# One ring of four double PSUM buffers in the attention stage, paired maxima, and regrouped weight steps

## The chip, the cores and the metric

The kernel runs on one core of a Trainium2 chip. The core has five engines with queues of their own: TensorE (PE in the profile, its weight loads PEld), VectorE (DVE), ScalarE (ACT), GpSimd (POOL) and SyncE (SP, which only issues transfers here). TensorE writes its results into PSUM, which has eight banks of 512 fp32 numbers in each of 128 partitions; the other engines read them there. The metric is the device time of one execution in microseconds (us), lower is better.

## The reference

```python
def _attn_ref(q, k, v):                     # 2 x 8 heads, 1152 keys, head_dim 64
    q_pool = q.reshape(B, H, S // 2, 2, D).mean(axis=3)      # 576 queries
    scores = scale * np.matmul(q_pool, k.transpose(0, 1, 3, 2))
    scores = scores - np.max(scores, axis=-1, keepdims=True)
    attn = np.exp(scores)
    attn = attn / (np.sum(attn, axis=-1, keepdims=True) + 1e-09)
    return np.matmul(attn, v)
...
x = attn_out                                # 1152 tokens x 512
g = np.maximum(x @ w_in, 0.0) ** 2          # 512 -> 2048
x = g @ w_out                               # 2048 -> 512
return (x @ w_a) * (x @ w_b) @ w_out2       # 512 -> 1536 -> 512
```

The weights are float64 and q, k, v float32; the output is float32.

## The kernel before

fp32 products are made of pieces: a number x is split into `hi` (x rounded to fp32r by ScalarE) and `lo` (x minus hi, by VectorE), and a product is hi·hi + hi·lo + lo·hi. float64 weights are brought to fp32 on the chip by integer operations (`w_stage`).

**Units.** Attention runs over 8 pairs of heads p (tile halves of 64 partitions, one head each) and two halves of the 576 queries: 16 units n = 2p + c of 288 queries. A unit does this, and the order in which the code is written is the order on every engine, since the schedule is manual:

- `scores(n, t)` for nine blocks of 128 keys: eight matmuls of 288 columns into one double buffer `ps` (a bank for each head); the last two add the negated row maxima (`mrow`). ScalarE makes `e` = exp(ps), and GpSimd adds the `e` up (`acc`; in the last unit VectorE does). VectorE adds the last two blocks (`sum_last`), GpSimd adds that to `acc` at the start of the next unit (`sum_end`).
- Between the score rounds, `max_pair(p+1, j, c)` makes scores of the *next* pair, for the row maxima alone: two matmuls of 384 columns (one head each), and VectorE reduces each to a column (`colmax`). There are six such pairs in a unit, nine in unit 1, none in units 14 and 15.
- `prep(p+2, odd)` transposes the keys and queries of the pair after the next into `pt` and splits them: 8 blocks in even units, 7 in odd ones (none from unit 12 on). `max_row` transposes the maxima (`mr`, copied to `mrow` by ScalarE). In odd units `max_mix` makes three more matmuls for maxima of the last queries.
- `values(n)`: 36 matmuls e·v into `po`; ScalarE copies the result to `xf`.
- `scale(n-2)`: VectorE's reciprocal of the sums `sg` and the product with `xf`. `denom(n-1)`: `acc` summed over partitions by TensorE (`den`), copied to `sg` by ScalarE. `x_split(n-3)` splits the finished output into `xh` and `xl`.
- In units 12 to 15, `w_step` prepares the first four weight tiles in three stages each: stage 0 is L129 (ScalarE) and L131 (VectorE), stage 1 is L135 and L138 (VectorE) and, at the next step, L119 (ScalarE), stage 2 is L153 (VectorE).

After unit 15, `early_mm(f)` and `early_post(f)`, f = 0 to 3, make the first products of the feed-forward part (tiles `e`, 24 matmuls of 288 columns each) from outputs of the first batch, into buffers of the same PSUM pool; ScalarE frees them with `r` (L563). Then come the two feed-forward parts, in which TensorE is busy nearly without a gap.

**Start.** Before unit 0 the keys of pair 0 come in three blocks of 384 (`pk`): three transposes, `prep_hi`, three `max_pair`, `prep_lo`. Then `max_end`, `prep(1, 0)`, `prep(1, 1)` and `max_row(0)`.

**PSUM.** Two pools share the eight banks:

```python
ps_s = es.enter_context(tc.tile_pool(name="ps_s", bufs=2, space=PSUM))
ps_m = es.enter_context(tc.tile_pool(name="ps_m", bufs=4, space=PSUM))
```

`ps_s` has two double buffers (`two_banks`): `ps`, `pt`, `po`, `pk` and the early products `e`. `ps_m` has four single ones: the scores for maxima `pm`, `mr` and `den`. A new tile takes a buffer of its pool that is free in program order, and its first matmul waits until the last reader of the old tile is done. Which instruction waits for which is fixed when the program is built: before, score round t waits for the exponential of round t-2, and a pair of `pm` for the maxima of two pairs earlier.

## Time and profile before

| | |
|---|---|
| time, median of 3 runs | 678.01 us (676.39 to 678.29) |
| the profiled execution | 679.79 us, of which 677.6 us is the span of the trace |
| TensorE busy in the span | 659.6 us (97%) |
| VectorE, ScalarE, GpSimd busy | 456.2, 310.5 and 195.9 us |
| attention up to the first early product | 245.3 us of the span |
| transfers | 52.90 MB, 78 GB/s on average |

Busy time of TensorE counts a matmul from its start to the modelled end of its pipeline, so that it overlaps with the next; it shows a short wait hardly at all. What TensorE lost is read from the starts of its instructions in the timeline, and from the granted clock, which has two levels here: 1.00 (2.4 GHz) and half of it (1.2 GHz).

### The profile page before, as it was taken

What the parts mean: (1) busy time and instruction counts of PE and PEld (TensorE: products, weight loads), DVE (VectorE), ACT (ScalarE), POOL (GpSimd) and SP (SyncE); (2) the same over time, 40 slices, a digit from 0 to 9 for tenths busy, and PEclk for the clock granted to TensorE, in tenths of its full rate; (3) what the DMA queues carried; (4) which work ended last, traced back from release to release, by engine and by line L of the source; (5) the groups of instructions that cost most, each with busy time, mean ns of one, the idle gap of its engine ahead of it and who ended that gap; (6) DMA issues with size and microseconds to landing.
All of it is one profiled execution on the core that took longest, in us unless ns stands there. A gap on an engine that the chain in (4) does not pass through costs nothing.

```text
span 677.6 us, 11443 instructions
## 1 busy us (share of the span) xinstructions
PE 659.6 (97%) x4614; PEld 586.2 (87%) x4614; DVE 456.2 (67%) x808; ACT 310.5 (46%) x571; POOL 195.9 (29%) x157
## 2 busy tenths in 40 slices
PE   6999999999998989999999999999999999999997
PEld 4777777777766669999999999999999889999986
DVE  5777888888799796894249874576777312777311
ACT  1454566566654745672247652334555222555100
POOL 1477889889887610320000000000000000000000
PEclk8699999999998998999999999999999999999999
DMA  7704034041031120322224321323434210441022
GB/s 174 176 1 106 12 96 107 1 105 37 2 129 32 33 63 27 123 86 86 85 62 125 95 63 62 94 94 94 125 124 127 91 31 1 124 125 63 17 63 62
DMA packets 55541, 52.90 MB, mean 78 GB/s; under 512 B 20416, under 2 KB 49344, under 8 KB 55488
## 3 DMA queue, kind: packets, MB, share of 16 engines
q1 hardware_dynamic: 55280, 51.58, 26.9%
q8 instruction: 36, 0.59, 0.4%
q10 hardware_dynamic: 208, 0.59, 0.3%
q14 instruction: 17, 0.14, 0.1%
HBM read 49.81 MB, written 2.36 MB: 77 GB/s over the span
## 4 chain that ended last, share of the span: by engine, by line
PE 89%; DVE 6%; ACT 3%; DMA 1%; issue 0%; ACTq 0%; DVEq 0%
PE ps L374 12%; PE po L400 9%; PE y L546 5%; PE y L544 5%; PE y L545 5%; PE h L546 4%; PE h L544 4%; PE h L545 4%; PE a L544 4%; PE b L544 4%; PE a L545 4%; PE b L545 4%; PE a L546 4%; PE b L546 4%; PE o L545 4%; PE o L546 4%
## 5 line engine op out<-in xcount | busy, mean ns | idle before, releaser
L386 POOL TENSOR_TENSOR acc<-acc,e 128x576 f32<-128x576 f32 x75 | 107.8, 1437 | 5.9
L318 DVE TENSOR_REDUCE mm<-pm 128x1 f32<-128x384 f32 x192 | 93.9, 549 | 18.9 <-PE pm L325 18.4
L379 ACT ACTIVATE e<-ps 128x576 f32<-128x576 f32 x144 | 92.7, 652 | 28.5 <-PE ps L374 23.9
L153 DVE TENSOR_TENSOR wlo<-wx,whi 128x512 fp32r<-128x512 f32 x60 | 42.4, 707 | 54.2 <-ACT whi L119 54.2
L400 PE MATMUL po<-e,vin 128*64 128x288 f32 x576 | 73.4, 409 | 0.0
L119 ACT CAST whi<-wx 128x512 fp32r<-128x512 f32 x68 | 42.2, 620 | 60.6 <-DVE wx L138 60.6
L544 PE MATMUL y<-gh,whi 128*128 128x384 f32 x192 | 64.6, 336 | 0.0
L546 PE MATMUL y<-gh,wlo 128*128 128x384 f32 x192 | 64.5, 336 | 0.0
L545 PE MATMUL y<-gl,whi 128*128 128x384 f32 x192 | 64.5, 336 | 0.0
L400 PEld LDWEIGHTS po<-e,vin 128*64 128x64 f32 x576 | 39.9, 137 | 27.7 <-issue 1.5
L374 PE MATMUL ps<-hi 64*128 64x288 f32 x288 | 55.2, 365 | 2.9 <-ACT e L379 1.6
L546 PE MATMUL h<-xh,wlo 128*128 128x384 f32 (+1 forms) x176 | 57.5, 327 | 0.0
L545 PE MATMUL h<-xl,whi 128*128 128x384 f32 (+1 forms) x176 | 57.5, 327 | 0.0
L544 PE MATMUL h<-xh,whi 128*128 128x384 f32 (+1 forms) x176 | 57.5, 327 | 0.0
L687 DVE TENSOR_TENSOR t<-b,as 128x384 f32<-128x384 f32 x36 | 20.1, 558 | 46.2 <-PE b L546 46.2
L138 DVE SCALAR_TENSOR_TENSOR wx<-raw,wx 128x512 int32<-128x512 int32 x68 | 49.3, 725 | 2.4
L374 PEld LDWEIGHTS ps<-hi 64*128 64x128 f32 x288 | 28.7, 189 | 23.3 <-ACT e L379 14.8
L546 PE MATMUL a<-yh,wlo 128*128 128x384 f32 x144 | 48.1, 334 | 0.0
L544 PE MATMUL a<-yh,whi 128*128 128x384 f32 x144 | 48.1, 334 | 0.0
L545 PE MATMUL a<-yl,whi 128*128 128x384 f32 x144 | 48.1, 334 | 0.0
L544 PE MATMUL b<-yh,whi 128*128 128x384 f32 x144 | 48.1, 334 | 0.0
L545 PE MATMUL b<-yl,whi 128*128 128x384 f32 x144 | 48.1, 334 | 0.0
(109 smaller groups left out, 1592.0 us busy)
## 6 DMA issues: line engine op xcount, KB each, us to landing
raw<-in_moe_w_out_dram SPq DMA_DIRECT2D x28, 512.0 KB, 3.4
raw<-in_moe_w_in_dram SPq DMA_DIRECT2D x16, 512.0 KB, 3.8
raw<-in_moe_w_a_dram SPq DMA_DIRECT2D x12, 512.0 KB, 3.5
raw<-in_moe_w_b_dram SPq DMA_DIRECT2D x12, 512.0 KB, 3.6
vin<-in_v_dram SPq DMA_DIRECT2D x8, 576.0 KB, 4.2
qin<-in_q_dram SPq DMA_DIRECT2D x7, 576.0 KB, 6.3
kin<-in_k_dram SPq DMA_DIRECT2D x14, 288.0 KB, 5.3
out_dram<-oacc SPq DMA_DIRECT2D x5, 192.0 KB, 2.2
```

The lines of the kernel that those rows point to most:

```text
L119: nc.scalar.copy(w["hi"], w["x"].bitcast(F32))
L138: nc.vector.scalar_tensor_tensor(out=x, in0=high.bitcast(I32), scalar=-(2 ** 31), in1=x, op0=ALU.bitwise_and, op1=ALU.bitwise_or)
L153: eng.tensor_tensor(out=lo, in0=x.bitcast(F32), in1=hi.bitcast(F32), op=ALU.subtract)
L318: nc.vector.tensor_reduce(out=mm[p][:, i, c:c + 1], in_=ps[:, :MC], op=ALU.max, axis=AX.X)
L374: nc.tensor.matmul(ps[:, a, :CQ], w, m, start=i == 0, stop=i == 3)
L379: nc.scalar.activation(ex[u, t], ps[:, :, :CQ], AF.Exp, scale=SCALE)
L386: eng.tensor_tensor(out=acc[u], in0=acc[u], in1=ex[u, t], op=ALU.add)
L400: nc.tensor.matmul(po[r, 0, :CQ], vin[u // 2][:, a, t, :], ex[u, t][:, a, :], start=t == 0, stop=t == KT - 1)
L544: nc.tensor.matmul(ps, lh, rh, start=i == 0, stop=False)
L545: nc.tensor.matmul(ps, lh, rl, start=False, stop=False)
L546: nc.tensor.matmul(ps, ll, rh, start=False, stop=i == n - 1)
L687: nc.vector.tensor_tensor(out=t, in0=pab[1][:, :CW], in1=a, op=ALU.mult)
```

## The change

One pool of four double buffers takes the place of the two pools. `max_pair` writes both heads into the two banks of one buffer, and one reduction of VectorE gives both maxima; `max_mix` takes two buffers instead of three. The three first blocks of keys each ask for a tile of their own, `max_end` for pair 0 stands ahead of the last `prep_lo`, and `max_row(0)` between the two halves of `prep(1, ·)`. In the last units the weight steps are spread otherwise, `scale(13)` and `denom(14)` stand earlier in unit 15, and `scale(14)` follows its `values`.

```diff
-            ps_s = es.enter_context(tc.tile_pool(name="ps_s", bufs=2, space=PSUM))
-            ps_m = es.enter_context(tc.tile_pool(name="ps_m", bufs=4, space=PSUM))
+            ps_s = es.enter_context(tc.tile_pool(name="ps_s", bufs=4, space=PSUM))
...
             def colmax(p, i, c, ps):
+                nc.vector.tensor_reduce(out=mm[p][:, i, c], in_=ps, op=ALU.max, axis=AX.X)
+
+            def max_pair(p, j, c):
...
-                nc.vector.tensor_reduce(out=mm[p][:, i, c:c + 1], in_=ps[:, :MC], op=ALU.max, axis=AX.X)
...
-                    ps = [ps_m.tile([P, 512], F32, tag="m", name=f"pm{p}_{j}{a}_{c}") for a in range(2)]
...
-                    for a in range(2):
-                        colmax(p, 2 * j + a, c, ps[a])
...
+                ps = two_banks(f"pm{p}_{j}_{c}")
+                for a, r in enumerate(halves):
+                    nc.tensor.matmul(
+                        ps[:, a, :MC], hi[p][r, S + j * P:S + (j + 1) * P], hi[p][r, c * MC:(c + 1) * MC],
+                        start=True, stop=True,
+                    )
+                colmax(p, slice(2 * j, 2 * j + 2), c, ps[:, :, :MC])
+
+            def max_mix(p):
+                for cs in ((0, 1), (2,)):
+                    ps = two_banks(f"px{p}_{cs[0]}")
+                    for i, c in enumerate(cs):
+                        nc.tensor.matmul(ps[:, i, :MC], qm[p % 2], hi[p][:, c * MC:(c + 1) * MC], start=True, stop=True)
+                    colmax(p, 2 * NQ, slice(cs[0], cs[-1] + 1), ps[:, :len(cs), :MC])
...
-                pt = ps_m.tile([P, 512], F32, tag="m", name=f"mr{u}")
+                pt = two_banks(f"mr{u}")[:, 0]
...
-                pt = ps_m.tile([P, 512], F32, tag="m", name=f"den{u}")
+                pt = two_banks(f"den{u}")[:, 0]
...
-            pk = two_banks("pk")
-            for c in range(2):
+            for c in range(MX):
                 one = [K[3 * c:3 * c + 3]]
-                prep_t(0, pk, c, one[0])
-                prep_hi(0, pk[:, c:c + 1], one)
+                pk = two_banks(f"pk{c}")
+                prep_t(0, pk, 0, one[0])
+                prep_hi(0, pk, one)
                 max_first(c)
-                prep_lo(0, pk[:, c:c + 1], one)
-            pk = two_banks("pk2")
-            prep_t(0, pk, 0, K[6:])
-            prep_hi(0, pk, [K[6:]])
-            max_first(2)
-            prep_lo(0, pk, [K[6:]])
+                if c < MX - 1:
+                    prep_lo(0, pk, one)
             max_end(0, 0)
-            rests = [prep(1, g) for g in range(2)]
+            prep_lo(0, pk, one)
+            rests = [prep(1, 0)]
             max_row(0)
+            rests.append(prep(1, 1))
...
+                if n == NU - 1:
+                    scale(n - 2)
...
-                if n >= NU - 4:
+                for _ in range(min(2, n - NU + 5)):
                     w_step(NE)
-                    w_step(NE)
+                end = n == NU - 1
+                if end:
+                    denom(n - 1)
                 values(n)
-                scale(n - 2)
-                denom(n - 1)
+                scale(n - 1 if end else n - 2)
+                if not end:
+                    denom(n - 1)
...
-                if n >= NU - 4:
+                for _ in range(min(2, n - NU + 4)):
                     w_step(NE)
-            scale(NU - 2)
```

The new waits, as the built program has them: the keys' second block takes the buffer of the first pair of maxima and waits for that pair's reduction (before: for `prep_lo` of the first block, which stands behind six reductions), and the third block likewise. In a unit, score rounds 2, 5 and 8 wait for the exponentials of rounds 0, 3 and 6; rounds 3, 4, 6 and 7 wait for the reductions of pairs 0, 1, 2 and 3 of the same unit; the pairs wait for exponentials. In odd units `po` waits for ScalarE's copy `mrow`, whose buffer it takes. In units 14 and 15, which have no maxima, round t waits for the exponential of round t-4. Of the early products, f = 1, 2 and 3 wait for the copies of unit 14's sums, unit 15's outputs and unit 15's sums, and none for another's `r`.

**VectorE, start** (`pm` scores for maxima, `mm` the maxima, `lo` the low parts, `nmw` the negated row maxima; the last two numbers before the buffer's own are pair of tiles and block of keys). Before, from the second block on:

```order
L296 TENSOR_TENSOR lo0_160<-pk_173,hi0_159 128x384
L318 TENSOR_REDUCE mm0_182<-pm0_00_2_226 128x1
L318 TENSOR_REDUCE mm0_182<-pm0_01_2_227 128x1
L318 TENSOR_REDUCE mm0_182<-pm0_10_2_232 128x1
L318 TENSOR_REDUCE mm0_182<-pm0_11_2_233 128x1
L318 TENSOR_REDUCE mm0_182<-pm0_20_2_238 128x1
L318 TENSOR_REDUCE mm0_182<-pm0_21_2_239 128x1
L296 TENSOR_TENSOR lo0_160<-pk2_221,hi0_159 128x384
L346 TENSOR_REDUCE nmw0_95<-mm0_182 128x6
```

and of the change, on the same engine at the same place:

```order
L295 TENSOR_TENSOR lo0_157<-pk1_189,hi0_156 128x384
L315 TENSOR_REDUCE mm0_175<-pm0_0_2_212 128x2
L315 TENSOR_REDUCE mm0_175<-pm0_1_2_216 128x2
L315 TENSOR_REDUCE mm0_175<-pm0_2_2_220 128x2
L344 TENSOR_REDUCE nmw0_92<-mm0_175 128x6
L295 TENSOR_TENSOR lo0_157<-pk2_207,hi0_156 128x384
```

Six reductions of one column each became three of two columns, and the row maxima now stand ahead of the last low part.

**VectorE, from unit 12 to the maxima of unit 13** (`e2` the sum of the last two blocks, `wx` a weight tile being prepared, `sg` the sums of a unit, `xf` its outputs). Before:

```order
L390 TENSOR_TENSOR e2_12_2839<-e12_6_2798 128x576
L131 TENSOR_SCALAR wx0_2847<-raw0_2843 128x512
L131 TENSOR_SCALAR wx1_2853<-raw1_2849 128x512
L424 RECIPROCAL sg10_2693<-sg10_2693 128x288
L425 TENSOR_TENSOR xf10_2482<-xf10_2482,sg10_2693 128x288
L135 SCALAR_TENSOR_TENSOR wx0_2847<-wa0_2845,wx0_2847 128x512
L138 SCALAR_TENSOR_TENSOR wx0_2847<-raw0_2843,wx0_2847 128x512
L318 TENSOR_REDUCE mm7_2711<-pm7_20_0_2903 128x1
```

and of the change:

```order
L388 TENSOR_TENSOR e2_12_2643<-e12_6_2606 128x576
L131 TENSOR_SCALAR wx0_2651<-raw0_2647 128x512
L422 RECIPROCAL sg10_2509<-sg10_2509 128x288
L423 TENSOR_TENSOR xf10_2312<-xf10_2312,sg10_2509 128x288
L315 TENSOR_REDUCE mm7_2523<-pm7_2_0_2693 128x2
```

One weight step instead of three stands ahead of unit 13's first maxima; the other two went to units 13 and 14.

**VectorE, from unit 14's sum to the sums of unit 15** (`acc15`, which `den15` on TensorE waits for, and behind it the early products; `wlo` a finished weight tile's low part). Before:

```order
L390 TENSOR_TENSOR e2_14_3196<-e14_6_3167 128x576
L131 TENSOR_SCALAR wx2_3202<-raw2_2885 128x512
L131 TENSOR_SCALAR wx3_3206<-raw3_2887 128x512
L424 RECIPROCAL sg12_3086<-sg12_3086 128x288
L425 TENSOR_TENSOR xf12_2874<-xf12_2874,sg12_3086 128x288
L135 SCALAR_TENSOR_TENSOR wx2_3202<-wa2_3200,wx2_3202 128x512
L138 SCALAR_TENSOR_TENSOR wx2_3202<-raw2_2885,wx2_3202 128x512
L384 TENSOR_TENSOR acc15_3264<-e15_0_3252 128x576
```

and of the change:

```order
L388 TENSOR_TENSOR e2_14_2983<-e14_6_2954 128x576
L153 TENSOR_TENSOR wlo0_2840<-wx0_2651,whi0_2839 128x512
L153 TENSOR_TENSOR wlo1_2875<-wx1_2831,whi1_2874 128x512
L422 RECIPROCAL sg12_2867<-sg12_2867 128x288
L423 TENSOR_TENSOR xf12_2672<-xf12_2672,sg12_2867 128x288
L131 TENSOR_SCALAR wx2_3020<-raw2_2835 128x512
L131 TENSOR_SCALAR wx3_3024<-raw3_2837 128x512
L422 RECIPROCAL sg13_3016<-sg13_3016 128x288
L423 TENSOR_TENSOR xf13_2860<-xf13_2860,sg13_3016 128x288
L382 TENSOR_TENSOR acc15_3050<-e15_0_3038 128x576
```

Two low parts of weights and the reciprocal and product of unit 13 now stand ahead of unit 15's sums, and one stage of a weight (L135, L138) stands behind them.

## Rows read from the trace of the kernel before

**Rows 1.** Timeline of the start: start us, length us, engine, line, instruction, [idle before it]
```profile
10.22 2.88 DVE L318 TENSOR_REDUCE mm<-pm 128x1 f32<-128x384 f32 x6
...
13.62 0.90 PE L272 MATMUL pk<-idf,kin 128*128 128x128 f32 x3 [1.89 <-DVE lo L296]
...
15.81 2.88 DVE L318 TENSOR_REDUCE mm<-pm 128x1 f32<-128x384 f32 x6 [2.24 <-PE pm L325]
...
22.96 0.16 DVE L346 TENSOR_REDUCE nmw<-mm 128x6 fp32r<-128x18 f32 x1
...
23.42 1.17 PE L272 MATMUL pt<-idf,qs 96*128 96x96 f32 x6
...
25.72 0.61 PE L374 MATMUL ps<-hi 64*128 64x288 f32 x2 [0.62 <-DVE lo L296]
```

**Rows 2.** Transfers of the first 40 us: busy tenths, one digit for each us
```profile
DMA  0029999717999996000199999999999600000000
```

**Rows 3.** Instructions grouped by line and shape, start to 262 us: count, busy us, mean ns
```profile
L296 DVE TENSOR_TENSOR lo<-pt,hi 128x1024 fp32r<-128x1024 f32 x7 | 8.6, 1225 | 10.8 <-ACT hi L292 10.8
```

**Rows 4.** Timeline of unit 7, an odd one, up to unit 8's first score
```profile
123.16 0.40 PE L374 MATMUL ps<-hi 64*128 64x288 f32 x2
...
123.79 0.34 PE L325 MATMUL pm<-hi 64*128 64x384 f32 x2
...
124.08 1.28 ACT L379 ACTIVATE e<-ps 128x576 f32<-128x576 f32 x2 [0.30 <-POOL acc L394]
...
124.22 1.94 DVE L318 TENSOR_REDUCE mm<-pm 128x1 f32<-128x384 f32 x4
...
124.78 0.19 PEld L374 LDWEIGHTS ps<-hi 64*128 64x128 f32 x2 [0.23 <-ACT e L379]
...
129.47 0.40 PE L374 MATMUL ps<-hi 64*128 64x288 f32 x2
...
131.74 0.42 ACT L365 CAST mrow<-mr 128x288 fp32r<-128x288 f32 x1
131.82 4.08 PEld L400 LDWEIGHTS po<-e,vin 128*64 128x64 f32 x36 [0.24 <-issue]
...
136.82 0.40 PE L374 MATMUL ps<-hi 64*128 64x288 f32 x2
```

**Rows 5.** Stretches (unit 0, units 12 and 13, early products): busy us, then granted clock, DMA share, GB/s
```profile
25.72:40.52 14.80, 14.71 (x135) 11.57 (x135) 10.55 (x22) 7.12 (x12) 11.02 (x10) 0.89 0.45 105
...
191.10:203.60 12.50, 12.45 (x131) 9.08 (x129) 11.34 (x18) 8.53 (x16) 10.43 (x8) 1.00 0.54 175
203.60:220.20 16.60, 14.87 (x134) 11.27 (x132) 15.29 (x27) 7.72 (x15) 12.78 (x10) 0.90 0.11 33
...
245.30:262.20 16.90, 14.63 (x99) 14.40 (x98) 12.63 (x15) 6.38 (x13) 1.62 (x2) 0.90 0.11 32
```

**Rows 6.** Timeline of VectorE ahead of the maxima of unit 13
```profile
206.00 1.82 DVE L138 SCALAR_TENSOR_TENSOR wx<-raw,wx 128x512 int32<-128x512 int32 x1
207.75 2.86 DVE L318 TENSOR_REDUCE mm<-pm 128x1 f32<-128x384 f32 x6
```

**Rows 7.** Timeline of TensorE at the same place
```profile
208.34 0.91 PE L325 MATMUL pm<-hi 64*128 64x384 f32 x2 [1.71 <-DVE mm L318]
```

**Rows 8.** Timeline of VectorE in units 14 and 15 and behind them
```profile
222.83 1.91 DVE L153 TENSOR_TENSOR wlo<-wx,whi 128x512 fp32r<-128x512 f32 x1
...
237.17 6.34 DVE L386 TENSOR_TENSOR acc<-acc,e 128x576 f32<-128x576 f32 x7
...
244.76 0.68 DVE L153 TENSOR_TENSOR wlo<-wx,whi 128x512 fp32r<-128x512 f32 x1
245.36 1.95 DVE L424 RECIPROCAL sg<-sg 128x288 f32<-128x288 f32 x1
247.34 0.46 DVE L425 TENSOR_TENSOR xf<-xf,sg 128x288 f32<-128x288 f32 x1
```

**Rows 9.** Timeline of TensorE in the early products
```profile
254.18 0.45 PE L544 MATMUL e<-xh,whi 128*128 128x288 f32 x1 [2.27 <-ACT r L563]
```

More of the change, by code (lines that the diff above doesn't have):

```diff
@@ L315, in colmax @@
             def colmax(p, i, c, ps):
+                nc.vector.tensor_reduce(out=mm[p][:, i, c], in_=ps, op=ALU.max, axis=AX.X)
+            def max_pair(p, j, c):
                 if p not in mm:
                     mm[p] = ap.tile([P, 2 * NQ + 1, MX], F32, tag="mm", bufs=2, name=f"mm{p}")
-                nc.vector.tensor_reduce(out=mm[p][:, i, c:c + 1], in_=ps[:, :MC], op=ALU.max, axis=AX.X)
-            def max_pair(p, j, c):
-                if p < NPR:
-                    ps = [ps_m.tile([P, 512], F32, tag="m", name=f"pm{p}_{j}{a}_{c}") for a in range(2)]
-                    for a, r in enumerate(halves):
-                        nc.tensor.matmul(
-                            ps[a][:, :MC], hi[p][r, S + j * P:S + (j + 1) * P], hi[p][r, c * MC:(c + 1) * MC],
-                            start=True, stop=True,
-                        )
-                    for a in range(2):
-                        colmax(p, 2 * j + a, c, ps[a])
-            def max_mix(p, c):
-                if p < NPR:
-                    ps = ps_m.tile([P, 512], F32, tag="m", name=f"pm{p}_x_{c}")
-                    nc.tensor.matmul(ps[:, :MC], qm[p % 2], hi[p][:, c * MC:(c + 1) * MC], start=True, stop=True)
-                    colmax(p, 2 * NQ, c, ps)
+                ps = two_banks(f"pm{p}_{j}_{c}")
[11 more added lines that the diff above has]
+                    colmax(p, 2 * NQ, slice(cs[0], cs[-1] + 1), ps[:, :len(cs), :MC])
             def max_end(p, c):
@@ L502, in attention @@
                 m = 0 if n == 0 else p + 1
-                if odd or not n:
-                    for c in range(MX):
-                        max_mix(m, c)
-                    if m < NPR:
-                        max_end(m, 1)
+                if (odd or not n) and m < NPR:
+                    max_mix(m)
+                    max_end(m, 1)
                 if n < NU - 1:
```

## Prediction

> **What bounds the kernel now.** I read the page first: TensorE is busy nearly throughout, and behind the early products it runs without a gap, so that the change can gain only in the 262 us ahead of that point. There I read the starts of TensorE's instructions in the timeline, stage by stage, and the granted clock of each stretch.
>
> Start. TensorE and VectorE wait for each other. The transpositions of the keys' second block start at 13.62, 1.89 us late, behind the first block's low part, which stands behind six reductions; VectorE then has nothing until 15.81, when the second round's scores are there. The last row maxima end at 23.12 (22.96 + 0.16), and unit 0's first score stands at 25.72 [rows 1]. The transfers of the start are over at about 16 us (a dip at 8 parts the first pair's from the second pair's); a later batch begins at 19 [rows 2].
>
> A unit. Scores are made in pace with ScalarE. In unit 7 the first round and its pair of maxima take TensorE 0.63 (123.16 to 123.79). The two exponentials take 0.64 each, and round 2 starts 0.06 behind the first one's end (124.08 + 0.64 = 124.72, and 124.78). Six more rounds take 129.47 - 124.78 = 4.69 us, 1.56 for two rounds [rows 4]. Three parts of those 1.56 are shown: 0.63 for a round's matmuls, 0.64 for the exponential, 0.06 for the release; the other 0.23 is the time from the last matmul to the exponential's start. So a cycle score, exponential, release goes round with two buffers, and its latency sets the pace; neither TensorE nor ScalarE is full.
>
> Units 12 and 13. Unit 13 takes 16.60 us against 12.50, at a granted clock of 0.90 against 1.00 [rows 5]. VectorE does weight steps until 207.75 and only then the maxima [rows 6]; TensorE waits 1.71 us for them, and starts again at half clock [rows 7].
>
> End of attention. VectorE's seven additions for unit 15's sums end at 237.17 + 6.34 = 243.51, a low part of a weight takes it 0.68 to 1.91 us, a reciprocal with its product 1.95 + 0.46 [rows 8]. The early products wait 2.27 us at the third tile for ScalarE [rows 9], and the stretch shows a clock of 0.90 again [rows 5].
>
> **The change, part by part.**
>
> The price of a paired reduction. No row shows one. From above: two single ones, 2 x 2.88 / 6 = 0.96 us [rows 1]. From below: VectorE reads 1024 fp32 numbers out of two banks in 1.225 us [rows 3], which for 768 is 0.92. I take 0.94; the same matmuls feed it.
>
> Pace of the rounds. A round now waits for an exponential three rounds back or for a reduction. Three rounds then take 0.63 + 0.23 + 2 x 0.64 + 0.06 = 2.20 us instead of 1.5 x 1.56 = 2.345, so the six rounds 4.40 instead of 4.69: -0.29 per unit. Do the reductions hold this up? The first starts 124.22 - 123.16 = 1.06 behind the unit's first score [rows 4], ends at 2.00, and the second at 2.94; by my pace round 3 comes at 2.26 and round 4 at 2.96. That just fits. A reduction of 0.94 in a stretch of 2.20 / 3 x 1.5 (two of three rounds have a pair: 1.10 per pair) keeps up; longer than that and VectorE would be the pace.
>
> Odd units. `po` now waits for `mrow`. It starts 131.82 - 123.16 = 8.66 behind the unit's start; `mrow` ends at 131.74 + 0.42 - 123.16 = 9.00 [rows 4]. The maxima move with the rounds, so `po` comes at 9.00 - 0.29 + 0.06 = 8.77: +0.11 for the unit in place of -0.29. Behind `po` on TensorE's queue are the sums and the next unit's scores; they all move with it. In even units `po` waits for the fifth pair's reduction, done before.
>
> Start. With own buffers the second block's transpositions wait only for the first pair's reduction (10.22 + 0.94 = 11.2) instead of 13.62. From transpositions to the first reduction it takes 15.81 - 13.62 = 2.19 [rows 1], so the second round could be reduced from 13.4 on, while VectorE is at the first until 10.22 + 2.82 + a low part of 384 columns (384 / 1024 x 1.225 = 0.46, [rows 3]) = 13.5. VectorE becomes continuous: two more rounds of 2.82 with a low part between give 13.5 + 2.82 + 0.46 + 2.82 = 19.6, and with the row maxima 19.8 instead of 23.12. Behind them TensorE has `mr` (25.72 - 0.62 - 24.59 = 0.5, with 24.59 the end of the last transpositions), then the seven blocks of the second half of `prep` (1.17 for six, about 1.3), then unit 0: 21.7 instead of 25.72, -4.0. Bounds: if `prep` is in the way as now, only the 3.3 of the maxima; if `mr` and the blocks overlap, -4.6. The second pair's keys are needed at about 18 instead of 21 to 22; the transfers that bring them have ended by 16 [rows 2].
>
> Units 0 and 1. Unit 0 has the same rounds and fewer pairs in the way: -0.15 (half a unit's gain). Unit 1 has nine pairs, set by VectorE: nine times at most 0.02 to 0.04, -0.3.
>
> Units 2 to 12, even: 6 x -0.29 = -1.75. Odd, 3 to 11: 5 x +0.11 = +0.55.
>
> Unit 13. One weight step instead of three stands ahead of its first maxima; the wait of 1.71 goes [rows 7], and with it the half clock (0.10 x 16.60 = 1.66, [rows 5]). With the pace's -0.29 that makes 12.9; a plain odd unit less 0.29 is 13.4, unit 12 less 0.29 is 12.2. I take 12.7: -3.9 (bounds -3.2 and -4.4). The steps taken away fall into units 13 and 14, behind the maxima, where VectorE has room.
>
> Units 14, 15 and the early products. Unit 14 and 15 have no maxima, and round t waits for the exponential of t-4, so TensorE runs ahead by up to 2 us a unit. That buys nothing if unit 15's sums come late, and VectorE's chain to them grows: from unit 14's last sum on it gets two low parts (0.68 to 1.91 each) and a reciprocal with its product (2.41), and loses one stage of a weight (two instructions, about as long as two low parts of 0.68) [rows 8]. That is +2.4 to +4.9 us. Exponentials that come about 1.2 earlier take back a part, ScalarE's copy for a weight, now ahead of unit 14's, gives that away again. With 2.4 the sums are there at 243.51 + 2.4 = 245.9 less what all units ahead gained, and the first early product, now some 1.8 behind them (245.3 - 243.51), at 247.7: 2.4 late. Behind that the third tile no longer waits for ScalarE's `r`: -2.27 [rows 9]. The half clock, which now follows that wait (0.10 x 16.9 = 1.7, [rows 5]), would follow the new one instead, since TensorE then stands idle for 3 to 4 us ahead of the sums. Reciprocals that stood in the early products are over earlier, which may free another 0.4: -0.3 (from -3, if the low parts are short and the exponentials early, to +2, if they take 1.91 each).
>
> Sum: -4.0 - 0.15 - 0.3 - 1.75 + 0.55 - 3.9 - 0.3 = -9.85, so 679.8 - 9.9 = 669.9 for the profiled execution. The runs' median lies 1.8 below that one's time before, so 668.2 us.
>
> **Rivals.**
>
> The reductions become the pace, and the kernel slower. Rounds 3, 4, 6 and 7 wait for them, which they never did. Round 7 needs four of them: 1.06 + 4D + 0.06 behind the unit's first score, for a reduction of D. By my pace it comes at 1.62 + 5 x 2.20 / 3 = 5.29 (1.62 is round 2's start), so the two are equal at D = 1.04. Each further 0.1 costs 0.4 a unit in fourteen units and 0.9 for the nine reductions of the start, 6.5 in all; with the 0.9 that the start loses on the way to 1.04, the gains are used up near D = 1.18. At D = 1.4 the time is 668.2 + 0.9 + 3.6 x 6.5 = 692. For it: no row shows a paired reduction, and the row that I lean on is of another operation. Against: it reads 1024 numbers, more than a pair has, in 1.225, and two single reductions are 0.96 [rows 1, 3].
>
> The start gains nothing, because the second pair's keys arrive late or `prep` is in the way: 668.2 + 4.0 = 672.2. For it: the dip and the batches show that keys arrive in order and late in the stretch. Against: they have ended 2 us before they are needed [rows 2].
>
> The end gets worse. The low parts take 1.91 and ScalarE's copy holds unit 14's exponentials: the sums come not 2.4 but 4.9 late, and 1 to 2 more for the copy, so 668.2 + 2.5 + 1.5 = 672.2, or 673 if the half clock lasts longer. For it: a row at 1.91 stands in that stretch; against: one at 0.68 as well [rows 8].
>
> More gain: TensorE's clock. In unit 0 the granted clock is 0.89 over 14.80 us [rows 5], so 1.6 us are lost to half clock behind the gaps of the start; with closer work the full clock could come earlier, and at the end the halving could stay away (1.7): 668.2 - 1.6 - 1.7 = 664.9. The Trainium skill, "TensorE: Matmul & The Clock Gate", Part 1, says that the slow clock is the default state and activity releases it. By that rule a denser start would win up to 1.6 more and unit 13 its full clock; the same rule speaks against the change at the end, where TensorE's idle time is gathered in one place. In this trace unit 13 with its 1.71 of waiting shows 0.90 and unit 12 without one 1.00, which agrees.
>
> **How the numbers follow.** Main case 0.70 (its own range 665 to 671), more gain 0.10, start without gain 0.07, worse end 0.07, slower 0.06. The range from 662.5 to 673.5 holds all but the slow case and the tails. A measurement of this kernel tells 0.3%, 2 us, from no change. Faster than 676 is all but the slow case and its borders: 0.90; within 2 us 0.05; slower 0.05.
>
> **What the profile after would show.** Right: a paired reduction of 0.92 to 0.96; the first score of unit 0 near 21.7 and VectorE hardly idle between 10 and 20; even units near 13.0, odd ones near 13.8 with `po` waiting for `mrow`; unit 13 near 12.7 at full clock; TensorE waiting 2 to 4 us for unit 15's sums, and not at the third early tile. Wrong: score rounds that wait for `mm`, a reduction over 1.04, or a first score still behind 24.

## The result and the profile after

The changed kernel takes 668.24 us (median of 4 runs, 667.91 to 668.79) against 677.38 us (4 runs), a ratio of 0.9866 with a 95% interval of 0.9848 to 0.9884. The forecast was 668.2. Its profiled execution is the one of 667.91 us, with a span of 666.1; the profiled execution before was the one of 679.79 us, 2.4 above the median before, so that the table below shows 2.4 us more of a difference than the medians do.

The page, busy time of each engine and share of the span:

```profile
PE 649.5 (98%) x4614; PEld 581.9 (87%) x4614; DVE 453.3 (68%) x704; ACT 307.7 (46%) x571; POOL 198.3 (30%) x157
```

TensorE's busy time fell by 10.1 us for the same matmuls; that figure shows short waits hardly at all, so I read the stages by the first score of each unit, in both timelines:

| stage | before | after | difference | forecast |
|---|---|---|---|---|
| start, up to unit 0 | 25.72 | 20.20 | -5.52 | -4.0 |
| unit 0 | 14.80 | 13.71 | -1.09 | -0.15 |
| unit 1 | 15.25 | 14.98 | -0.27 | -0.3 |
| units 2 to 12, even | 79.40 | 76.92 | -2.48 | -1.75 |
| units 3 to 11, odd | 68.43 | 68.83 | +0.40 | +0.55 |
| unit 13 | 16.56 | 12.75 | -3.81 | -3.9 |
| units 14, 15, early products | 42.01 | 43.28 | +1.27 | -0.3 |
| the rest | 415.43 | 415.43 | 0 | 0 |

The timeline of the start, VectorE and TensorE, against [rows 1] and two more lines of before:

```profile
6.91 0.95 DVE L253 TENSOR_TENSOR qs<-qin 96x768 f32<-96x768 f32 x1 [3.07 <-DMA qin<-in_q_dram]
...
19.70 2.88 DVE L318 TENSOR_REDUCE mm<-pm 128x1 f32<-128x384 f32 x6 [0.54 <-PE pm L325]
```

After:

```profile
5.54 0.95 DVE L252 TENSOR_TENSOR qs<-qin 96x768 f32<-96x768 f32 x1 [1.69 <-DMA qin<-in_q_dram]
...
8.88 2.69 DVE L315 TENSOR_REDUCE mm<-pm 128x2 f32<-128x768 f32 x3
...
9.90 0.55 PE L271 MATMUL pk<-idf,kin 128*128 128x128 f32 x3 [0.64 <-DVE mm L315]
...
11.95 2.68 DVE L315 TENSOR_REDUCE mm<-pm 128x2 f32<-128x768 f32 x3
...
15.16 2.69 DVE L315 TENSOR_REDUCE mm<-pm 128x2 f32<-128x768 f32 x3
...
17.88 0.17 DVE L344 TENSOR_REDUCE nmw<-mm 128x6 fp32r<-128x18 f32 x1
...
20.20 0.61 PE L372 MATMUL ps<-hi 64*128 64x288 f32 x2
```

The second block's transpositions wait 0.64 for the first pair's reduction and no longer for the low part. VectorE goes through three rounds without a gap, one every 3.1 to 3.2 us, where before there were 5.6 and 3.9. The first line is an accident of this execution: the first load landed at 5.54, before at 6.91. At the same landing the first score would stand at 21.57 (an estimate: 20.20 + 1.37), which is 4.15 earlier than before. Two later runs of the same start whose load landed at 6.82 and 6.91 have their first score at 21.25 and 21.54, which agrees; others that landed at 5.58 to 5.69 have it anywhere from 20.26 to 21.40, so tenths count for little here.

Unit 6, rounds 2 and 5 and the exponentials between them (rounds 2 to 4):

```profile
103.88 0.40 PE L372 MATMUL ps<-hi 64*128 64x288 f32 x2
...
104.71 1.92 ACT L377 ACTIVATE e<-ps 128x576 f32<-128x576 f32 x3 [0.27 <-PE ps L372]
...
106.01 0.40 PE L372 MATMUL ps<-hi 64*128 64x288 f32 x2
```

Three rounds take 106.01 - 103.88 = 2.13 us (forecast 2.20, before 2.35). Round 5 starts as soon as the exponential of round 3 is done, which is the second of the three and ends at about 105.96.

Unit 7, the odd unit of [rows 4]:

```profile
115.15 0.40 PE L372 MATMUL ps<-hi 64*128 64x288 f32 x2
...
115.78 0.34 PE L323 MATMUL pm<-hi 64*128 64x384 f32 x2
...
116.17 1.82 DVE L315 TENSOR_REDUCE mm<-pm 128x2 f32<-128x768 f32 x2 [0.85 <-PE pm L323]
...
123.41 0.42 ACT L363 CAST mrow<-mr 128x288 fp32r<-128x288 f32 x1
...
123.88 4.59 PE L398 MATMUL po<-e,vin 128*64 128x288 f32 x36 [0.31 <-ACT mrow L363]
...
128.88 0.40 PE L372 MATMUL ps<-hi 64*128 64x288 f32 x2
```

`po` waits for `mrow`, as forecast, and stands 8.73 behind the unit's first score (forecast 8.77, before 8.66).

Stretches of the changed kernel, columns as in [rows 5]: unit 0, units 12 to 15, early products.

```profile
20.20:33.91 13.71, 13.71 (x135) 10.88 (x134) 10.42 (x16) 7.83 (x13) 11.07 (x10) 0.93 0.55 129
182.56:194.64 12.08, 12.08 (x130) 9.00 (x129) 10.81 (x10) 7.82 (x15) 9.85 (x8) 1.00 0.57 180
194.64:207.39 12.75, 12.75 (x134) 9.41 (x132) 11.38 (x17) 7.82 (x15) 12.01 (x10) 1.00 0.01 1
207.39:219.14 11.75, 10.72 (x118) 8.06 (x116) 11.65 (x8) 7.63 (x16) 9.07 (x6) 1.00 0.24 68
219.14:235.73 16.59, 11.52 (x118) 7.99 (x117) 15.76 (x19) 6.83 (x14) 5.95 (x5) 0.94 0.05 17
235.73:250.67 14.94, 14.94 (x99) 14.94 (x97) 12.29 (x16) 7.32 (x14) 2.12 (x2) 0.84 0.22 71
```

Unit 13 is at full clock. What it gained stands in unit 15: VectorE is busy 15.76 of its 16.59 us and TensorE only 11.52. The timeline of VectorE and TensorE there, against [rows 8] and two more lines of before:

```profile
228.17 1.44 DVE L390 TENSOR_TENSOR e<-e 128x576 f32<-128x576 f32 x1 [3.43 <-ACT e L379]
229.54 3.17 DVE L131 TENSOR_SCALAR wx<-raw 128x512 int32<-128x512 uint32 x2
```

After:

```profile
216.69 1.96 DVE L388 TENSOR_TENSOR e<-e 128x576 f32<-128x576 f32 x1
218.57 3.74 DVE L153 TENSOR_TENSOR wlo<-wx,whi 128x512 fp32r<-128x512 f32 x2
...
224.61 0.75 DVE L131 TENSOR_SCALAR wx<-raw 128x512 int32<-128x512 uint32 x2
...
228.49 5.93 DVE L384 TENSOR_TENSOR acc<-acc,e 128x576 f32<-128x576 f32 x7
...
234.57 1.23 PE L409 MATMUL den<-acc,ones 128*64 128x288 f32 x4 [5.07 <-DVE acc L384]
```

The two low parts take 1.87 us each, the upper end of the forecast's bounds; the sums are late by 5.07, and the early products begin at half clock (0.84 over 14.94 us). The wait at the third early tile [rows 9] is gone. The long low parts are not the whole of it: the two weight stages L131 behind them took 0.75 instead of 3.17. From the start of unit 14's last sum (L388, before L390) to the end of the additions VectorE takes 17.7 us against 15.3. That sum itself starts 9.3 us behind unit 14's first score instead of 8.0, because VectorE is still at weight steps, where before it stood idle for 3.43 and waited for the exponential.

### The profile page after: what moved, and what is told of

Same layout as the page of the kernel before. It is cut to its first block, busy times and chain, and to the rows that moved or that the text cites. A ratio compares the mean times of both kernels' runs of the same rounds, so it can differ in the third digit from the quotient of the medians.

```text
span 666.1 us, 11343 instructions
## 1 busy us (share of the span) xinstructions
PE 649.5 (98%) x4614; PEld 581.9 (87%) x4614; DVE 453.3 (68%) x704; ACT 307.7 (46%) x571; POOL 198.3 (30%) x157
## 4 chain that ended last, share of the span: by engine, by line
PE 91%; DVE 6%; ACT 1%; issue 1%; POOL 0%; DVEq 0%; POOLq 0%
PE ps L372 11%; PE po L398 9%; PE y L542 5%; PE y L544 5%; PE y L543 5%; PE h L542 4%; PE h L544 4%; PE h L543 4%; PE a L542 4%; PE a L544 4%; PE b L544 4%; PE b L542 4%; PE a L543 4%; PE b L543 4%; PE o L544 4%; PE o L543 4%
## 5 line engine op out<-in xcount | busy, mean ns | idle before, releaser
L384 POOL TENSOR_TENSOR acc<-acc,e 128x576 f32<-128x576 f32 x75 | 109.9, 1465 | 5.9
L315 DVE TENSOR_REDUCE mm<-pm 128x2 f32<-128x768 f32 x96 | 88.2, 953 | 15.1 <-PE pm L323 14.2
L377 ACT ACTIVATE e<-ps 128x576 f32<-128x576 f32 x144 | 89.9, 655 | 16.9 <-PE ps L372 13.9
L372 PE MATMUL ps<-hi 64*128 64x288 f32 x288 | 50.0, 343 | 1.2 <-ACT e L377 1.0
L138 DVE SCALAR_TENSOR_TENSOR wx<-raw,wx 128x512 int32<-128x512 int32 x68 | 49.3, 725 | 2.4
L135 DVE SCALAR_TENSOR_TENSOR wx<-wa,wx 128x512 int32<-128x512 int32 x68 | 48.4, 711 | 0.0
```

The costliest lines, as they stand in the source:

```text
L135: nc.vector.scalar_tensor_tensor(out=x, in0=a.bitcast(I32), scalar=3, in1=x, op0=ALU.logical_shift_left, op1=ALU.bitwise_or)
L138: nc.vector.scalar_tensor_tensor(out=x, in0=high.bitcast(I32), scalar=-(2 ** 31), in1=x, op0=ALU.bitwise_and, op1=ALU.bitwise_or)
L315: nc.vector.tensor_reduce(out=mm[p][:, i, c], in_=ps, op=ALU.max, axis=AX.X)
L372: nc.tensor.matmul(ps[:, a, :CQ], w, m, start=i == 0, stop=i == 3)
L377: nc.scalar.activation(ex[u, t], ps[:, :, :CQ], AF.Exp, scale=SCALE)
L384: eng.tensor_tensor(out=acc[u], in0=acc[u], in1=ex[u, t], op=ALU.add)
```

## The experiments

All are edits of the changed kernel. One thing is needed to read them by less than 2 us: kernels whose code is the same up to unit 1 reached it between 33.91 us (the changed kernel) and 36.10. Their first load landed between 5.5 and 6.9, and unit 0 took them 13.71 to 15.02 us, at granted clocks from 1.00 down to 0.83. So I give each median, and beside it the part of the span from unit 1's first score on: 632.2 us in the changed kernel, 637.1 before. That part varies too, by about 1 us: the early products of the same code took 14.94 us at clock 0.84 in the changed kernel and 14.09 at 0.90 in the first run below.

**The start of before.** The first two blocks share `pk`, the last low part stands ahead of `max_end`, both halves of `prep` ahead of `max_row(0)`.

```diff
-            for c in range(MX):
+            pk = two_banks("pk")
+            for c in range(2):
...
-                pk = two_banks(f"pk{c}")
...
-            rests = [prep(1, 0)]
+            rests = [prep(1, g) for g in range(2)]
             max_row(0)
-            rests.append(prep(1, 1))
```

> The changed kernel with the start of before: the first two blocks of keys share a tile again, the last low part stands ahead of the row maxima, and both halves of prep ahead of the transposed maxima; ring, pairs and weight steps stay changed. Theory: of the 5.5 us by which unit 0's first score came earlier in the changed kernel's trace, 4.1 are the start's new order and 1.4 only that the first transfer had landed earlier in that execution; so the score comes 4.1 later than with own buffers, and the whole is 668.2 + 4.1 = 672.3 (up to 673.4, if unit 0's clock rises as late as before). Rival: the start's new order does nothing and the earlier transfer was all: 668 within 1.

Measured: 669.66 us (668.78 to 669.89), +1.4; 631.2 from unit 1. Neither theory. The intervals of the two ratios to before overlap (0.9858 to 0.9897, and 0.9848 to 0.9884), so that the trace says more than the median. The first load landed at 6.90 here, as before, so the start can be laid beside [rows 1] directly. Its timeline:

```profile
13.42 0.90 PE L271 MATMUL pk<-idf,kin 128*128 128x128 f32 x3 [2.84 <-DVE lo L295]
...
15.62 2.69 DVE L315 TENSOR_REDUCE mm<-pm 128x2 f32<-128x768 f32 x3 [2.25 <-PE pm L323]
...
16.64 0.90 PE L271 MATMUL pk<-idf,kin 128*128 128x128 f32 x3 [0.41 <-DVE mm L315]
...
18.84 2.69 DVE L315 TENSOR_REDUCE mm<-pm 128x2 f32<-128x768 f32 x3
...
23.21 0.40 PE L372 MATMUL ps<-hi 64*128 64x288 f32 x2
```

The second block waits for the low part again (2.84). But the third round follows 3.22 behind the second (3.89 before), because the third block takes a buffer of the ring and waits for a reduction; each round is 0.19 shorter; and the first score finds a free buffer without a wait (0.62 before). So of the 4.15 us, 25.72 - 23.21 = 2.5 come from ring and pairs, and 1.6 from the own buffers and the order, which this run does not tell apart.

**The weight steps of before** (with `scale` and `denom`) in units 12 to 15.

```diff
-                for _ in range(min(2, n - NU + 5)):
+                if n >= NU - 4:
                     w_step(NE)
...
+                    w_step(NE)
                 values(n)
-                scale(n - 1 if end else n - 2)
-                if not end:
-                    denom(n - 1)
+                scale(n - 2)
+                denom(n - 1)
...
-                for _ in range(min(2, n - NU + 4)):
+                if n >= NU - 4:
                     w_step(NE)
+            scale(NU - 2)
```

> The changed kernel with the weight steps, scale and denom of units 12 to 15 placed as before; ring, pairs and start stay changed. Theory: unit 13 loses its 3.8 us again because weight steps stand ahead of its maxima, and the end gets back the 1.3 that it lost by the late sums: 668.2 + 3.8 - 1.3 = 670.7. Rival: the deeper ring carries unit 13 over the weight steps, so that the new places cost only at the end: 667. Second rival: the end was not lost by the late sums but by the ring: 672.

Measured: 667.43 us (667.03 to 668.75), not later than the changed kernel; 630.9 from unit 1. The stretches of unit 13, unit 14, unit 15 and the early products:

```profile
195.37:212.65 17.28, 14.18 (x133) 10.91 (x131) 15.15 (x19) 7.43 (x14) 13.50 (x10) 0.90 0.10 31
212.65:223.14 10.49, 10.49 (x118) 8.01 (x116) 8.93 (x8) 8.35 (x17) 7.52 (x5) 1.00 0.17 52
223.14:236.93 13.79, 10.68 (x118) 7.82 (x116) 12.96 (x15) 6.34 (x13) 5.46 (x5) 1.00 0.13 39
236.93:249.76 12.83, 12.83 (x98) 12.83 (x97) 11.90 (x14) 6.46 (x13) 1.61 (x2) 1.00 0.15 42
```

and TensorE's two long waits in them:

```profile
200.88 0.61 PE L372 MATMUL ps<-hi 64*128 64x288 f32 x2 [3.10 <-DVE mm L315]
236.30 0.71 PE L409 MATMUL den<-acc,ones 128*64 128x288 f32 x4 [3.11 <-DVE acc L384]
```

Unit 13 is 4.5 us longer (the theory had 3.8). The end, however, is not 1.3 but 6.2 shorter: 37.11 us from unit 14's first score to the end of the early products, against 43.28 in the changed kernel and 42.01 before. So the regrouped weight steps only carried VectorE's work from ahead of unit 13's maxima to ahead of unit 15's sums, and TensorE's loss with it. (The first rival named 667, but for another reason: the ring did not carry unit 13 over the weight steps.) With the places of before, ring and pairs make the end 4.9 shorter; 2.1 of the 6.2 is the clock of the early products, 1.00 here and 0.84 in the changed kernel.

**Two single reductions on each pair.**

```diff
-                colmax(p, slice(2 * j, 2 * j + 2), c, ps[:, :, :MC])
+                for a in range(2):
+                    colmax(p, slice(2 * j + a, 2 * j + a + 1), c, ps[:, a:a + 1, :MC])
```

> The changed kernel with two reductions of one column each on every pair of maxima instead of one of two columns; the ring and all else stay. Theory: the pace is set by the release of buffers and not by the reductions, and two single ones take 0.96 to 1.02 us against 0.95, under the 1.04 from which they would hold the scores up: 668 within 2. Rival: the paired reduction is what gained in the start and in the units: 671 or more.

Measured: 671.82 us (671.42 to 672.20), +3.6; from unit 1 on +1.6. The rival is nearer. Odd units 3 to 13 became 0.10 to 0.42 longer, even ones from 2 to 12 by 0.06 to 0.11, unit 1 0.54. An odd unit, VectorE and TensorE:

```profile
119.77 1.94 DVE L315 TENSOR_REDUCE mm<-pm 128x1 f32<-128x384 f32 x4
...
124.26 0.41 PE L373 MATMUL ps<-hi 64*128 64x288 f32 x2 [0.16 <-DVE mm L315]
```

A score waits for `mm`, one of six that do in units 1 to 13; in the changed kernel none does. The price is now 1.02 for a pair by itself and 0.93 for each further pair right behind it, where the forecast had put the point at 1.04. Paired reductions take 0.95 for one and start 0.87 apart (1.82 for two).

**Every paired reduction twice.**

```diff
                 colmax(p, slice(2 * j, 2 * j + 2), c, ps[:, :, :MC])
+                colmax(p, slice(2 * j, 2 * j + 2), c, ps[:, :, :MC])
```

> The changed kernel with every paired reduction done twice (the second writes the same maxima), so that a pair costs VectorE 1.9 us instead of 0.95. By the prediction's rule for slow reductions (0.9 for the start's up to 1.04, and 6.5 us for each 0.1 above): 668.2 + 0.9 + 8.6 x 6.5 = 725, and score rounds 3, 4, 6 and 7 wait for the maxima. Rival: four buffers take up most of it and VectorE has room in a unit (11 of 13 us busy): below 690.

Measured: 734.0 us (733.61 to 735.79), 65.8 more; 686.9 from unit 1. TensorE's waits from 30 to 290 us (total, times, longest):

```profile
PE pm L323 <- DVE mm L315: 24.2, 36, 0.9
PE ps L373 <- DVE mm L315: 7.8, 10, 0.9
PE po L399 <- DVE mm L315: 4.8, 8, 1.2
```

It is mostly the pairs that wait, and not rounds 3, 4, 6 and 7. With two readers of each buffer of maxima the built program gives the buffers out otherwise than in the changed kernel: a pair mostly takes the buffer of the pair two earlier, and those rounds wait for exponentials. So this run does not try the rule's path. What sets the length shows in the stretches of an even unit, unit 6 of the changed kernel and unit 4 of this run (columns as in [rows 5]):

```profile
102.24:115.15 12.91, 12.91 (x138) 9.83 (x137) 10.57 (x11) 8.26 (x15) 12.52 (x10) 1.00 0.60 138
```

```profile
105.56:122.23 16.67, 13.79 (x139) 10.06 (x137) 16.43 (x17) 8.31 (x15) 12.23 (x9) 1.00 0.46 107
```

VectorE, busy 10.57 of 12.91 us there, is busy 16.43 of 16.67 here: the rival's room was there, some 2 us, the doubled reductions used it up, and the rest of their 5.9 us became the unit's. Units 3 to 9 became 3.8 longer, 12 and 13 5.1 to 5.3, the start and unit 1 8.8 and 10.1. That the rule came within 9 us of the time is luck.

**The ring alone**: single reductions, start and weight steps of before, in one kernel.

```diff
-                colmax(p, slice(2 * j, 2 * j + 2), c, ps[:, :, :MC])
+                for a in range(2):
+                    colmax(p, slice(2 * j + a, 2 * j + a + 1), c, ps[:, a:a + 1, :MC])
...
+            pk = two_banks("pk")
+            for c in range(2):
...
+                if n >= NU - 4:
                     w_step(NE)
+                    w_step(NE)
```

> The ring of four double buffers alone: two single reductions for each pair, and the start, the weight steps, scale and denom as before. Theory: the parts undone one by one simply add up (start +1.4, weight steps -0.8, single reductions +3.6), so 668.2 + 4.2 = 672.4 and the ring alone holds some 5.5 of the 9.5 us. Rival: the parts cover for each other (single reductions hurt more where the weight steps stand ahead of unit 13's maxima, and where the second round of maxima waits), 674 or more.

Measured: 673.99 us (673.87 to 674.02), ratio 0.9939 (0.9924 to 0.9954). The sum of the parts gives 672.4; single reductions behind the weight steps of before cost unit 13 more (18.53 us instead of 17.28). That is the rival's figure. So the ring alone holds about 4 of the 9 to 10 us. Most of the rest comes with the pairs: taking them out of the changed kernel cost 3.6. The end is 38.41 us here, 3.6 shorter than before, but unit 13 is 2.0 longer.

**Unit 15's sums early**, ahead of the weight steps and of unit 13's reciprocal.

```diff
-                if n == NU - 1:
-                    scale(n - 2)
...
+                if end:
+                    for _ in range(4):
+                        w_step(NE)
+                if n != NU - 2:
+                    for _ in range(min(2, n - NU + 5)):
+                        w_step(NE)
...
+            for u in (NU - 3, NU - 2):
+                scale(u)
```

> The changed kernel with VectorE's order in unit 15 changed alone: unit 15's sums stand right behind the reciprocal and product of unit 12, and ahead of the weight steps (two low parts, both tiles' later stages) and of unit 13's reciprocal, which follow them. Theory: the sums are then ready before TensorE comes to them; its wait of 5.07 us and the half clock behind it (0.06 of 16.6 and 0.15 of 16.3, together 3.4) go, and about 2 come back where the next part's first product waits for ScalarE, whose copies of the last outputs now come later: 668.2 - 5.1 - 3.4 + 2 = 661.7. Rival: the early products' own operands (low parts, copies) come late instead, so that the wait only moves: 666 or more.

Measured: 666.99 us (666.50 to 667.25); 629.3 from unit 1. The rival was right: the wait only moved. That for the sums fell from 5.07 to 1.23 and the early products ran at clock 1.00, but the next part's first product then waited for the third early tile's buffer:

```profile
249.22 0.40 PE L548 MATMUL h<-xh,whi 128*128 128x288 f32 x1 [2.44 <-ACT r L567]
```

Of the 6.5 us of the theory, 2.9 are left from unit 1 on.

**The same, with the last outputs' copies between the early products** (`scale`, `early_mm`, `early_post`, `x_split` in one loop).

```diff
-            scale(NU - 1)
-            x_split(NU - 3)
-            x_split(NU - 2)
-            x_split(NU - 1)
             for f in range(NE):
+                if f < 3:
+                    scale(NU - 3 + f)
                 early_mm(ps_s, f)
                 early_post(gpool, f)
+                if f < 3:
+                    x_split(NU - 3 + f)
```

> The same order of VectorE, and the last three reciprocals and copies of outputs spread between the early products, so that ScalarE reads the early products out before it waits for the last output. Theory: the 2 us that the former order loses at the next part's first product go too: 659.7. Rival: nothing waited there, and the two are equal within 1; or the copies of the outputs come too late for the products that read them: later than the former.

Measured: 667.91 us (667.60 to 668.65); 630.6 from unit 1, later than the former, as the second rival said. The first product came without a wait, 6.2 earlier behind unit 14's start than in the changed kernel, and the feed-forward part took 4.9 longer:

```profile
290.39 0.69 PE L547 MATMUL y<-gl,whi 128*128 128x384 f32 x1 [3.16 <-DVE gl L537]
```

The second product of the feed-forward part waits for VectorE's low parts `gl`, and runs at half clock behind that wait. The work that was put behind the sums is still ahead of those low parts on VectorE's queue.

**The transposed maxima after round 6 in odd units**, on top of that.

```diff
+                    if odd and t == 6:
+                        max_row(n + 1)
...
-                if n:
+                if n and not odd:
                     max_row(n + 1)
```

> The same again, and in odd units the transposed maxima are made after round 6 instead of after the last round, so that the values' buffer no longer waits for ScalarE's copy of them (0.32 us in seven units). Theory: 7 x 0.32 = 2.2 less: 657.5. Rival: ScalarE is then busy with that copy between two exponentials, and the last rounds come later by as much: equal within 1, or slower.

Measured: 666.59 us (666.05 to 667.08); 630.3 from unit 1. The odd units became 0.3 us shorter each (3 to 11: some 13.45 instead of 13.72), as in the theory, but the ring turned by one place and the first product of the next part met the last early tile's buffer:

```profile
247.18 0.45 PE L548 MATMUL h<-xh,whi 128*128 128x288 f32 x1 [3.87 <-ACT r L567]
```

**The first low parts on GpSimd**, in the changed kernel's order.

```diff
-            eng = nc.gpsimd if NE <= i < HF1 + 4 else nc.vector
+            eng = nc.gpsimd if i < HF1 + 4 else nc.vector
...
-                sum_end(n - 1)
+                if n < NU - 1:
+                    sum_end(n - 1)
...
+                if n == NU - 2:
+                    sum_end(n)
```

> The changed kernel with the low parts of the first four weight tiles made by GpSimd instead of VectorE (and GpSimd's last addition for unit 14 ahead of them); the order stays. Theory: not the order in unit 15 but VectorE's amount of work decides the end: with the sums early, the wait had only moved to the second product of the feed-forward part, which waits for VectorE's low parts of its input. With 5 us of work off its queue (3.74 ahead of unit 15's sums, 1.28 behind them) the wait of 5.07 falls to about 1.3 and no other takes its place; with part of the half clock 668.2 - 3.8 - 2 = 662.4. Rival: VectorE is slower while GpSimd works (1.87 us for a low part beside it, 0.65 alone), so that half of the gain goes: 665 or more.

Measured: 670.56 us (669.45 to 671.49), later; 634.1 from unit 1. Neither reason: a new wait took the old one's place.

```profile
226.76 2.42 DVE L131 TENSOR_SCALAR wx<-raw 128x512 int32<-128x512 uint32 x2 [3.33 <-POOL wlo L153]
...
238.38 1.23 PE L409 MATMUL den<-acc,ones 128*64 128x288 f32 x4 [7.28 <-DVE acc L384]
```

`wx` has two buffers; the next weight's first stage on VectorE now waits for GpSimd to have read the old one, and unit 15's sums stand behind it.

**Both of the last**, with the transposed maxima early up to unit 11 only.

```diff
+                    if odd and t == 6 and n < 12:
+                        max_row(n + 1)
...
-                if n:
+                if n and (not odd or n >= 12):
                     max_row(n + 1)
```

> The same, and in the odd units up to 11 the transposed maxima are made after round 6 (0.28 us a unit in the traces of the run that did it in all odd units). Theory: 6 x 0.28 = 1.7 less than the run without it: 660.7; the run that did it in all of them lost its gain at the feed-forward part's first product, which there waited 3.87 for the last early product's buffer, and here takes the first one's. Rival: it was the copy between the exponentials that lost it: equal within 1.

Measured: 669.31 us (668.75 to 670.36), 1.25 less than without the second edit; 631.95 from unit 1, 2.1 less. No wait at the next part's first product: the theory's step of 1.7, within what the runs can tell.

**Two more reciprocals on VectorE** behind the last `scale`.

```diff
             scale(NU - 1)
+            for i in range(2):
+                more = ap.tile([P, CQ], F32, tag="more", bufs=1, name=f"more{i}")
+                nc.vector.reciprocal(more, sg[NU - 1])
```

> The changed kernel with two more reciprocals on VectorE (3.9 us, into a tile that nothing reads) behind the last unit's scale, after all that the early products wait for. Theory: VectorE's queue from there to the second product of the feed-forward part has next to no slack in the changed kernel, so most of the 3.9 comes out at the end: 671 to 672. Rival: VectorE's idle gaps in that stretch (some 5 us in 244 to 272) take it up: 668 within 1.

Measured: 668.87 us (668.09 to 669.08), and 632.2 from unit 1, as in the changed kernel. The rival was right: the gaps that VectorE has between 243 and 255 us in the changed kernel (0.50, 0.93, 1.56 and 0.28, together 3.3) are gone here and took up most of the 3.9. In the changed kernel VectorE has slack there; in the order with the early sums it has next to none there.

**Together**: sums early, low parts on GpSimd behind them, transposed maxima early up to unit 11.

```diff
-            eng = nc.gpsimd if NE <= i < HF1 + 4 else nc.vector
+            eng = nc.gpsimd if i < HF1 + 4 else nc.vector
...
+                    if odd and t == 6 and n < 12:
+                        max_row(n + 1)
...
+                if end:
+                    for _ in range(4):
+                        w_step(NE)
...
+            for u in (NU - 3, NU - 2):
+                scale(u)
```

> What the runs pointed to, together: unit 15's sums ahead of the weight steps (as in the run with the sums early), the first four low parts on GpSimd, now behind those sums so that VectorE doesn't wait for them, and the transposed maxima after round 6 in odd units up to 11 (which also lets the next part's first product take the buffer of the first early one). Theory: from the 667.0 of the sums early, -1.5 for the odd units, -2.4 for the wait at the next part's first product, and VectorE's shorter queue keeps the second product from waiting in its place: 663. Rival: the work that was moved meets the second product's low parts all the same: 665.5, the gain of the odd units alone.

Measured: 664.74 us (663.86 to 665.63, 5 runs), a ratio to the kernel before of 0.9817 (0.9801 to 0.9833); 627.6 from unit 1, 4.6 less than the changed kernel, and between the two forecasts. The changed kernel's ratio is 0.9866 (0.9848 to 0.9884), so this one is the faster. No wait of TensorE stands between the early products and 300 us; the sums are late by 2.98, because VectorE's additions ran beside GpSimd's low parts (9.15 for seven, and 7.40 with the sums early alone, where the wait was 1.23):

```profile
223.39 9.15 DVE L384 TENSOR_TENSOR acc<-acc,e 128x576 f32<-128x576 f32 x7
...
226.68 3.52 POOL L153 TENSOR_TENSOR wlo<-wx,whi 128x512 fp32r<-128x512 f32 x2
...
232.69 1.23 PE L409 MATMUL den<-acc,ones 128*64 128x288 f32 x4 [2.98 <-DVE acc L384]
```

## Why the prediction was right

The time was right to a tenth of a microsecond, which is partly luck. The forecast for a profiled execution was 669.9, and it took 667.91: the table's terms add up to 1.65 more than forecast, since a load that landed early gave the start 1.37, unit 0 0.9 (its length varied by 1.3 us between runs of the same code) and the even units 0.7 more, against 1.6 less at the end. The medians differ by 9.1, where the forecast took 9.8 from a median of 678.0 that came out as 677.4.

*The paired reduction's price* (0.94) was right: 0.95.

*The pace of the rounds* (-0.29 a unit) was right in kind, and -0.41 in size. That a round waits for an exponential three rounds back was not quite right: rounds 2, 5 and 8 still wait for one two rounds back. What is gone is that wait in the other rounds, and none of those waited for a reduction.

*Odd units* (+0.11): +0.04 to +0.18, for the reason given, and the run with the maxima transposed earlier shows that the wait for `mrow` is what they lose.

*The start* (-4.0): about -4.15 at the same landing of the first load. The step said that own buffers bring it. The run with the old start gives them, with the new order, 1.4 to 1.6; the larger part is the third block's wait, the shorter rounds and the first score's buffer, which come with the ring and the pairs.

*Unit 13* (-3.9) was right as a length and wrong as a gain. The step said that the steps taken away "fall into units 13 and 14, behind the maxima, where VectorE has room". VectorE had too little: its queue ran full until unit 15's sums, and they came 5.07 late. With the old places unit 13 takes 4.5 more and the end 6.2 less, and the median is not higher. This regrouping brought nothing that the runs can tell.

*The end* (-0.3) was mis-sized by 1.6, in two terms. The first early product came 3.2 later behind unit 14's start, not 2.4. VectorE's chain from unit 14's last sum to the additions grew by 2.3, near the 2.4 of the forecast, but only because two misses cancel: the low parts took 1.87 each instead of 0.68, and the two stages L131 2.4 less than before. What the forecast left out is that this last sum itself would start 1.3 later and take 0.5 longer, behind the weight steps that had been moved (the additions, 0.4 shorter, and the step to the first product, 0.5 shorter, gave some of it back). And the early products gained 1.9 instead of 2.7, since half clock cost them 0.16 x 14.94 = 2.4 instead of 1.7. The term also hid two large ones of opposite sign, -4.9 with the ring, the pairs and the places of before, and +6.2 from the regrouping, of which the forecast had only the net; by the run of the ring alone the first is -3.6.

*Maxima as the pace* was rightly given a small chance, but its point (D = 1.04) was too high: single reductions, at 1.02 for a pair, already made six scores wait and cost 3.6 us, 1.6 of it from unit 1 on. At 0.95 none waits, so the point lies somewhere between, and the forecast stood some hundredths of a microsecond per reduction away from it. The text's own start of round 3, 2.26, would put round 7 at 2.26 + 4 x 2.20 / 3 = 5.19 and the point at 1.02. The doubled reductions say nothing of it, since there VectorE's whole work fills the unit.

*More gain by the clock*: unit 0's clock did rise earlier in the profiled execution (0.93 against 0.89), but over the runs of the same code it was anywhere from 0.83 to 1.00; the end's did not (0.84).

## What to carry to other kernels

A stall that is removed by moving work of a busy engine is removed only if that engine has a gap where the work goes; follow its queue up to the next thing that another engine waits for, and further, before the gain is counted (here unit 13's 3.8 us came back as a wait of 5.07, and that, when removed, as 2.44 and 3.16 further on). When several edits come together, undo them one at a time: the sum was right here with two of its parts credited to the wrong edit. With a ring that all stages share, moving one request turns the ring for all that follow, and doubling one reader gave the buffers out otherwise, so the waits have to be listed again for each order, that of an experiment too.

## What the runs showed of the hardware

VectorE is slowed by GpSimd, and not in all its operations. A low part of 128x512 took 1.87 us beside GpSimd's additions (218.57, above) and 0.68 alone [rows 8]; seven additions of 128x576 took 5.93 alone and 9.15 beside GpSimd. The weight stage L131, which has one input, took 3.17 for two beside GpSimd and 0.75 alone. Paired reductions out of PSUM took 0.95 throughout, and the reciprocal of one operand 1.94 to 1.96 in either case. The Trainium skill, "GPSIMD Engine Reference", section 1, says that GpSimd shares its SBUF interfaces with VectorE and contends with VectorE's instructions in a 2-port perf mode or with two SBUF inputs. The rows of two inputs agree; whether L131 was in such a mode no run here shows. So the subtraction that was moved to GpSimd for relief slowed the additions that it was to bring forward (9.15 instead of 7.40).

PSUM was read by VectorE and ScalarE alone in these runs; every operand of a GpSimd instruction is a tile in SBUF.

The granted clock in unit 0 is not a property of the code: with the same instructions up to there it was 0.93 in the changed kernel (13.71 us) and 0.83 in the run with the sums early, whose row is

```profile
21.08:36.10 15.02, 15.02 (x135) 12.32 (x134) 10.33 (x16) 7.96 (x13) 11.29 (x10) 0.83 0.51 119
```

The landing of the first load alone does not decide it: over runs of this code it was 0.93 at 5.54, 0.83 at 6.46, 1.00 at 6.82 and 0.90 at 6.91. What does was not tried, and stays open.
